# Low-rank factors loaded after batch 0's Q and K, and the last output tile stored in two halves

## The chip, the cores and the metric

The kernel runs on 1 core of one Trainium2 chip. The metric is the device time of the program in microseconds, lower being better; the time given for a kernel is the median of its runs.

## The reference

Sliding-window causal attention over 8 batches, 8 heads, 576 tokens and 64 dimensions a head, and then a mixer: a low-rank product over the tokens and a channel MLP. All inputs and the output are float32.

```python
def _attn_ref(q, k, v):                      # 8, 8, 576, 64
    scores = (1.0 / np.sqrt(D)) * np.matmul(q, k.transpose(0, 1, 3, 2))
    rel = pos[:, None] - pos[None, :]
    scores = np.where((rel >= 0) & (rel < 64), scores, -1000000000.0)
    attn = softmax(scores)
    return np.matmul(attn, v)

def _moe_ref(x, U, V, w_ch1, w_ch2):         # x: 8, 576, 512; U: 576, 32; V: 32, 576
    h = x.transpose(0, 2, 1) @ U @ V
    u = x + h.transpose(0, 2, 1)
    return u + np.maximum(u @ w_ch1, 0.0) @ w_ch2    # 512 -> 2048 -> 512
```

The MLP has by far the most products: 4608 tokens through 512 x 2048 and back.

## The kernel before

All products are in bf16; the loads by POOL's queue (GpSimd) turn float32 into bf16 on the way. Attention goes batch by batch; the MLP goes in 9 chunks of 512 tokens (c = 0 to 8), which don't line up with the batches of 576.

**Attention of a batch.** Q and K are brought into a transposed form, kt and qt: for batches 0 and 1 by TensorE transposes (`TK`, `TQ`, L258, with copies from PSUM at L269 and L274), for batches 2 to 7 by DMA transposes that SP issues (`TX`, L280). `SC(j)` makes the scores of two heads (L311) and their Exp on ScalarE (L329), in batch 0 with the mask added on TensorE (L305). `SC8` does the last block of all heads. `PV(t)` makes the output of token tile t (L364), divided by the sums on VectorE (DVE, L373 and L374) into x. Then comes the low-rank product: `UM` multiplies by U (L396, reading ub) and copies the result to hh on ScalarE (L406); batch 0's `HT` multiplies hh by V (L464, reading vrep), added in PSUM to the transposed x (`XT`, L447), and copies it to uTc, the transposed input of the MLP. `VM` makes the same sum untransposed, un (L486, L499). `UT(t)` transposes a tile of un into uTc where no `HT` did: by TensorE for batches 1 and 2 (L518, copied at L521 by ScalarE), by DMA for the rest (L514).

**MLP of a chunk.** `ch1(i)`, i = 0 to 15, makes 128 hidden channels with 4 matmuls of 512 columns (L560, weights w1b) and a Relu on ScalarE or DVE. `ch2(t, quarter)` sums 16 matmuls of 512 columns for token tile t (L582, weights w2b) into psU; after the fourth quarter DVE adds un (L591) into osb, and SP issues one store of 128 x 512 floats (L594).

**The order.** It is written out by hand. The 32 calls of a chunk's MLP are slots; tables (`PLACE`, `PLACE_1`, `PLACE_2`) say after which slot each piece of the next batch's attention is issued. Chunk 0 carries batch 1, chunk 1 carries batch 2, and so on; in chunk 1, `"VP"` and `"UTP"` place the last steps of batch 1: un (slots 0 to 4) and the transpose of its last tile (slot 5, `"UTP": [5]`). The scores of batch 2 are at slots 6, 6, 9, 9 and 11. Each engine runs its instructions in the order of issue.

**The start.** POOL's queue gets, in order: batch 0's K and Q in two halves of 4 heads each (L117: K, Q, K, Q), its V (L135, L140), the weights w1b in two halves (L211), then copies inside SBUF that shift V (L149, L152), batch 1's Q, K and V, and w2b (L219). SP's queue begins with the low-rank factors: U is loaded twice, in two arrangements of rows (uf0 and uf1, 4 DMAs at L199 to L204), V four times (vf, L208). Batch 0's attention runs alone, before any MLP; `turn_over` puts in matmuls with an unread result (L635). Its order on TensorE is this list, with `SC8` behind it:

```python
    for what in ("K0", "K1", "Q0", "Q1", "S0", "S1", "K2", "K3", "Q2", "Q3", "S2", "S3"):
```

After it, ScalarE casts the factors to bf16:

```python
    for i in range(2):
        nc.scalar.copy(out=ub[i][:], in_=uf[i][:])
    nc.scalar.copy(out=vrep[:, W : W + S], in_=vf[:])
```

and then PV, XT and U of batch 0 follow tile by tile, then the copies of hh, then HT. In batch 0 the copies of K2 and K3 from PSUM and all four of Q are on DVE.

Of the kernel before, what the change touches and what calls it, by code (L numbers as in the profile page):

```python
# [9 lines left out]
ALU = mybir.AluOpType  # L10

BF16 = mybir.dt.bfloat16
FP32 = mybir.dt.float32
# [3 lines left out]
def kernel(  # L17
# [11 lines left out]
    nc = tc.nc  # L29
    B, H, S, D = q.shape  # L30
    DM = H * D
    R = moe_U.shape[1]
    F = moe_w_ch1.shape[1]
    P = nc.NUM_PARTITIONS
    W = 64
# [3 lines left out]
    NFC = F // P  # L39
# [6 lines left out]
    NFULL = S // P  # L46
    CH = 512
    TPC = CH // P
    NTOK = B * S
    NCH = NTOK // CH  # L50
# [6 lines left out]
    outf = out.rearrange("b s m -> (b s) m")  # L57
# [7 lines left out]
    out_pool = ctx.enter_context(tc.tile_pool(name="osb", bufs=4))  # L65
# [3 lines left out]
    psum = {  # L69
        "mm": first.enter_context(tc.tile_pool(name="ps_t0", bufs=2, space=bass.MemoryType.PSUM)),  # L70
        "spare": first.enter_context(tc.tile_pool(name="ps_s0", bufs=1, space=bass.MemoryType.PSUM)),
    }
# [8 lines left out]
    w2b = const.tile([P, NFC, DM], BF16, name="w2b")  # L81
    NT = 5
    uf = [const.tile([P, NT, R], FP32, name=f"uf{i}") for i in range(2)]
    ub = [const.tile([P, NT, R], BF16, name=f"ub{i}") for i in range(2)]
    vrep = const.tile([P, W + S + W], BF16, name="vrep")
    vf = const.tile([P, S], FP32, name="vf")
# [59 lines left out]
    def shift_v(b, copy, tiles):  # L146
# [14 lines left out]
        out=ident[:],  # L161
        in_=ident[:],
# [11 lines left out]
    for n, base, step, mult in ((0, 0, 1, -1), (1, -1, -1, 1), (1, W, 1, -1)):  # L174
        nc.gpsimd.affine_select(
            out=maskA[:, 0, n, :],
            in_=maskA[:, 0, n, :],
# [9 lines left out]
    load_v(0)  # L187
    nc.vector.memset(vrep[:, 0:W], 0.0)
    nc.vector.memset(vrep[:, W + S : W + S + W], 0.0)
    nc.vector.memset(uf[0][:, NT - 1, :], 0.0)  # L190
    nc.vector.memset(uf[1][:, 0, :], 0.0)
    nc.vector.memset(xs[0][W:P, NT - 1, :, :], 0.0)
    nc.vector.memset(xs[1][0:W, 0, :, :], 0.0)
    for i in range(2):
# [1 line left out]
        nc.vector.memset(qn[i][W:P, NFULL, :, :], 0.0)  # L196


    nc.sync.dma_start(  # L199
        out=uf[0][:, 0:NFULL, :], in_=moe_U[0 : NFULL * P, :].rearrange("(c p) r -> p c r", p=P)  # L200
    )
    nc.sync.dma_start(out=uf[0][0:W, NFULL, :], in_=moe_U[NFULL * P : S, :])
    nc.sync.dma_start(out=uf[1][W:P, 0, :], in_=moe_U[0:W, :])
    nc.sync.dma_start(  # L204
        out=uf[1][:, 1:NT, :], in_=moe_U[W:S, :].rearrange("(c p) r -> p c r", p=P)
    )
    for g in range(4):
        nc.sync.dma_start(out=vf[g * R : (g + 1) * R, :], in_=moe_V[:, :])  # L208
    w1v = moe_w_ch1.rearrange("(c p) n -> p c n", p=P)
    for lo, hi in ((0, 1024), (1024, 2048)):  # L210
        nc.gpsimd.dma_start(out=w1b[:, :, lo:hi], in_=w1v[:, :, lo:hi])  # L211
# [11 lines left out]
    u_tiles = {}  # L223
    uT_tiles = {}

    def uT_of(c):
        if c not in uT_tiles:
            uT_tiles[c] = uT_pool.tile([P, TPC, NDC, P], BF16, name="uTc")
        return uT_tiles[c]
# [322 lines left out]
    def mlp(c):  # L552
        uTc = uT_of(c)
        c1 = [None] * NFC

        def ch1(i):
            def f():
                ps = psum["mm"].tile([P, CH], FP32, name="psA", tag="mm")
                for dc in range(NDC):
                    nc.tensor.matmul(  # L560
                        ps[:],
                        w1b[:, dc, i * P : (i + 1) * P],
                        uTc[:, :, dc, :],
                        start=(dc == 0),
                        stop=(dc == NDC - 1),
                    )
                c1[i] = c1_pool.tile([P, CH], BF16, name=f"c1_{i}")
                if i in (DVE_RELU if c > 0 else DVE_RELU_0):
                    nc.vector.tensor_relu(out=c1[i][:], in_=ps[:])  # L569
                else:  # L570
                    nc.scalar.activation(out=c1[i][:], in_=ps[:], func=ACT.Relu)
            return f

        acc = {}

        def ch2(t, quarter):
            def f():
                g = c * TPC + t
                if quarter == 0:
                    acc[t] = psum["mm"].tile([P, DM], FP32, name="psU", tag="mm")  # L580
                for i in range(4 * quarter, 4 * quarter + 4):
                    nc.tensor.matmul(  # L582
                        acc[t][:],
                        c1[i][:, t * P : (t + 1) * P],
                        w2b[:, i, :],
                        start=(i == 0),
                        stop=(i == NFC - 1),
                    )
                if quarter == 3:
                    osb = out_pool.tile([P, DM], FP32, name="osb")  # L590
                    nc.vector.tensor_tensor(  # L591
                        out=osb[:], in0=acc[t][:], in1=u_tiles[g][:], op=ALU.add
                    )
                    nc.sync.dma_start(out=outf[g * P : (g + 1) * P, :], in_=osb[:])  # L594
            return f

        return [ch1(i) for i in range(NFC)] + [ch2(t, r) for t in range(TPC) for r in range(4)]


# [19 lines left out]
    PLACE_2 = {  # L619
        "S": [6, 6, 9, 9, 11],  # L620
        "VP": [0, 1, 2, 2, 3, 4, 4, 4],
        "UTP": [5],
        "PV": [14, 14, 16, 16, 18],
        "TX": [12, 13, 14, 15, 16],
        "U": [19],
# [7 lines left out]
    def turn_over(n, cols=CH):  # L633
        for _ in range(n):
            nc.tensor.matmul(  # L635
                unread[:, 0:cols], idle[:, 0:P], idle[:, 0:cols], start=True, stop=True
            )
# [6 lines left out]
        out=maskA[:, 0, 2, :],  # L644
        in0=maskA[:, 0, 1, :],
# [7 lines left out]
        out=maskA[:, 0, 3:7, :].rearrange("p (o n) w -> p o (n w)", o=2),  # L653
        in_=pair.to_broadcast([P, 2, 2 * W]),
# [3 lines left out]
        out=maskB[:],  # L658
        in0=maskA[:, 0, :, :],
# [5 lines left out]
    for what in ("K0", "K1", "Q0", "Q1", "S0", "S1", "K2", "K3", "Q2", "Q3", "S2", "S3"):  # L665
        j = int(what[1])
        if what[0] == "S":
            a["S"][j]()
        else:
            a["T"][2 * j + (what[0] == "Q")]()  # L670
        turn_over({"K1": 3, "Q1": 1, "S0": 1, "K3": 1, "Q3": 1}.get(what, 0))
    a["S"][HP]()
    nc.vector.tensor_copy(out=maskA[:, 1, :, :], in_=maskA[:, 0, :, :])
# [19 lines left out]
    for c in range(NCH):  # L693
# [32 lines left out]
        for fill, extra in zip(mlp(c) + [lambda: None], slots):  # L726
            fill()
            for f in extra:
                f()
# [30 lines left out]
```

The softmax here doesn't subtract the row's maximum and nothing guards it: scores larger than these inputs give would overflow.

## Time and profile before

| what | value |
|---|---|
| time, median of 3 runs | 329.75 us (329.72 to 330.7) |
| the profiled execution's own time | 330.06 us |
| its span, first to last instruction | 328.3 us |
| busy: TensorE matmul, DVE, ScalarE, POOL | 316.2, 172.2, 94.7, 102.9 us |
| TensorE clock granted, mean | 0.998 |
| chain that ended last, by engine | PE 86%, DVE 5%, ACT 3%, DMA 3% |
| bytes read from and written to HBM | 37.14 MB, 9.44 MB |
| first MLP matmul (L560) | 24.95 us after the span's start |
| last MLP matmul (L582) begins | 324.19 us |

The profile shows one execution. PE is TensorE's matmuls, PEld its weight loads, ACT is ScalarE, SP is the engine that issues stores and transposes; a name with q (SPq, POOLq) is an engine's sequencer, which issues DMAs. Times are microseconds from the start of the span. L12 is line 12 of the kernel. "Busy" is the union of an engine's instructions; a matmul of 512 columns lasts 380 ns, though the next begins 215 ns after it, since they are pipelined. A line of groups or of the timeline gives the start, the length, the engine, the line, output and inputs; in brackets stands the idle time of the engine ahead of it and what ended that. DMA queues: q0 is the queue of POOL, q1 that of SP; for each the page gives packets, megabytes and the share of 16 engines' time.

### The profile page before, as it was taken

How to read it: one execution, taken by the hardware profiler on the slowest of the kernel's cores; microseconds unless marked ns; L12 is line 12 of the kernel's file. 1: busy time of each engine (PE TensorE's matmuls, PEld its weight loads, DVE VectorE, ACT ScalarE, POOL GpSimd, SP SyncE). 2: the span in 40 equal slices, each digit the busy share in tenths (PEclk: the TensorE clock that was granted, in tenths of full speed). 3: DMA queues.
4: the chain of work that ended last, by engine and by line, in shares of the span. 5: the costliest groups of instructions: out<-in, count | busy, mean ns of one | idle time of the engine just before them, and what ended most of it. 6: DMA issues, size and time to landing. Idle time of an engine off the chain costs nothing.

```text
span 328.3 us, 6734 instructions
## 1 busy us (share of the span) xinstructions
PE 316.2 (96%) x2802; PEld 147.9 (45%) x2802; DVE 172.2 (52%) x308; ACT 94.7 (29%) x143; POOL 102.9 (31%) x134
## 2 busy tenths in 40 slices
PE   6889999989999999999999999999999999999995
PEld 2444544434454444444444444444444444444442
DVE  4564682378645844584548553765376425115211
ACT  3435641028223530344025401540063001301400
POOL 8591878536536855417700500000000000000000
PEclk9999999999999999999999999999999999999999
DMA  8999999999999999999996993354300330021011
GB/s 114 179 208 195 170 189 169 148 155 175 131 134 208 165 137 154 207 174 141 145 209 98 134 140 112 62 86 103 105 4 2 73 106 32 2 82 45 0 66 64
DMA packets 151871, 39.56 MB, mean 121 GB/s; under 512 B 140960, under 2 KB 146080, under 8 KB 151840
## 3 DMA queue, kind: packets, MB, share of 16 engines
q0 software_dynamic: 100096, 18.36, 78.9%
q1 hardware_dynamic: 51744, 20.77, 35.5%
q8 instruction: 22, 0.36, 0.5%
q14 instruction: 9, 0.07, 0.1%
HBM read 37.14 MB, written 9.44 MB: 142 GB/s over the span
## 4 chain that ended last, share of the span: by engine, by line
PE 86%; DVE 5%; ACT 3%; DMA 3%; issue 2%; POOL 1%; POOLq 0%
PE psU L582 38%; PE psA L560 34%; PE xr L364 4%; DMA qg<-in_q_dram 3%; PE sc L311 3%; ACT pts L329 3%; PE psv L486 2%; DVE pts L331 1%; PE pshh L396 1%; DVE un L499 1%; PE tpg L258 1%; PE psht L396 0%; PE psh L396 0%; PE tpu L518 0%; PE ua L447 0%
## 5 line engine op out<-in xcount | busy, mean ns | idle before, releaser
L560 PE MATMUL psA<-uTc,w1b 128*128 128x512 bf16 x576 | 133.7, 380 | 2.3 <-DVE uTc L473 0.4
L560 PEld LDWEIGHTS <-w1b 128*128 128x128 bf16 x576 | 53.3, 98 | 63.3 <-issue 2.9
L591 DVE TENSOR_TENSOR osb<-psU,un 128x512 f32<-128x512 f32 x36 | 24.8, 689 | 78.0 <-PE psU L582 78.0
L329 ACT ACTIVATE pts<-sc 128x1024 bf16<-128x1024 f32 x32 | 31.3, 1023 | 8.8 <-PE sc L311 7.3
L331 DVE TENSOR_TENSOR pts<-pts,maskA 128x1024 bf16<-128x1024 bf16 x28 | 19.3, 691 | 10.2 <-ACT pts L329 10.2
L135 POOL DMA_DIRECT2D vA_105<-in_v_dram x16 | 14.1, 885 | 29.4 <-DVE c_9_2735 L569 18.3
L499 DVE TENSOR_TENSOR un<-psv,xs_102 128x512 bf16<-128x512 f32 (+1 forms) x20 | 13.0, 683 | 10.4 <-PE psv L486 10.4
L135 POOL DMA_DIRECT2D vA_104<-in_v_dram x16 | 14.1, 887 | 13.4 <-PE xr L364 7.9
L499 DVE TENSOR_TENSOR un<-psv,xs_103 128x512 bf16<-128x512 f32 (+1 forms) x20 | 13.0, 684 | 8.6 <-PE psv L486 8.4
L364 PEld LDWEIGHTS <-pts 128*64 128x64 bf16 x512 | 11.2, 110 | 10.4 <-issue 4.1
L126 POOL DMA_DIRECT2D kn_108<-in_k_dram x15 | 12.7, 847 | 10.1 <-DMA vA_105<-in_v_dram 5.8
L126 POOL DMA_DIRECT2D qn_110<-in_q_dram x15 | 12.7, 848 | 8.7 <-DMA qn_110<-in_q_dram 4.5
L126 POOL DMA_DIRECT2D kn_109<-in_k_dram x15 | 12.8, 857 | 6.4 <-DMA vA_104<-in_v_dram 3.9
L373 DVE RECIPROCAL rcp<-xr 128x8 f32<-128x8 f32 (+1 forms) x40 | 8.2, 204 | 12.8 <-PE xr L364 12.4
L311 PEld LDWEIGHTS <-kf 64*64 64x64 bf16 x704 | 10.1, 107 | 10.2 <-issue 9.1
L374 DVE TENSOR_TENSOR xs_103<-xr,rcp 128x512 bf16<-128x512 f32 (+1 forms) x20 | 13.8, 692 | 0.7
L374 DVE TENSOR_TENSOR xs_102<-xr,rcp 128x512 bf16<-128x512 f32 (+1 forms) x20 | 13.8, 690 | 0.7
L126 POOL DMA_DIRECT2D qn_111<-in_q_dram x15 | 12.8, 855 | 2.8 <-DMA qn_111<-in_q_dram 2.1
L486 PE MATMUL psv<-hh,vrep 128*128 128x512 bf16 x40 | 12.6, 379 | 0.0
L311 PE MATMUL sc<-qf,kf 64*64 64x128 bf16 (+1 forms) x576 | 11.2, 214 | 0.0
L635 PE MATMUL unread<-idle 128*128 128x512 bf16 x16 | 6.4, 524 | 1.3 <-DVE idle L156 1.3
L364 PE MATMUL xr<-vA_105,pts 128*64 128x65 bf16 x160 | 7.2, 197 | 0.2 <-DVE xs_103 L374 0.2
(553 smaller groups left out, 510.0 us busy)
## 6 DMA issues: line engine op xcount, KB each, us to landing
out_dram<-osb SPq DMA_DIRECT2D x36, 256.0 KB, 3.0
vA_104<-in_v_dram POOLq DMA_DIRECT2D x16, 128.0 KB, 8.1
w1b<-in_moe_w_ch_dram POOLq DMA_DIRECT2D x2, 1024.0 KB, 15.0
vA_105<-in_v_dram POOLq DMA_DIRECT2D x16, 128.0 KB, 11.5
w2b<-in_moe_w_ch_dram POOLq DMA_DIRECT2D x4, 512.0 KB, 12.6
kn_108<-in_k_dram POOLq DMA_DIRECT2D x12, 128.0 KB, 11.9
qn_110<-in_q_dram POOLq DMA_DIRECT2D x12, 128.0 KB, 13.2
kn_109<-in_k_dram POOLq DMA_DIRECT2D x12, 128.0 KB, 10.8
```

The lines of the kernel that those rows point to most:

```text
L126: nc.gpsimd.dma_start(out=dst[0:rows, t, :, :], in_=src[b, :, t * P : t * P + rows, :].rearrange("h p d -> p h d"),)
L135: nc.gpsimd.dma_start(out=va[:, t, :, 0:D], in_=v[b, :, t * P : (t + 1) * P, :].rearrange("h p d -> p h d"),)
L311: nc.tensor.matmul(sc[r0 : r0 + W, g, col * W : (col + n) * W], keys_of(j, u, rs), queries_of(j, blk, n, rs), start=not spare, stop=last o ...
L329: nc.scalar.activation(out=dst, in_=sc[:], func=ACT.Exp, scale=scale)
L331: nc.vector.tensor_tensor(out=dst, in0=dst, in1=maskA.rearrange("p g n w -> p g (n w)"), op=ALU.mult)
L364: nc.tensor.matmul(xr[r0 : r0 + W, h // 4, (h % 4) * VW : (h % 4 + 1) * VW], pts[:, h // 2, h % 2, blk, :] if blk < NB - 1 else ptl[:, h / ...
L374: nc.vector.tensor_tensor(out=x[lo:hi, t, :, :].rearrange("p (a h) d -> p a h d", a=2), in0=xv[:, :, :, 0:D], in1=rcp[lo:hi].to_broadcast( ...
L486: nc.tensor.matmul(ps[0][:, n, :], vrep[:, off : off + P], hh["sb"][:], start=True, stop=True)
L499: nc.vector.tensor_tensor(out=u_tiles[g][rs, :], in0=ps[0][rs, n, :], in1=x[rs, t, :, :].rearrange("p h d -> p (h d)"), op=ALU.add,)
L560: nc.tensor.matmul(ps[:], w1b[:, dc, i * P : (i + 1) * P], uTc[:, :, dc, :], start=(dc == 0), stop=(dc == NDC - 1),)
L582: nc.tensor.matmul(acc[t][:], c1[i][:, t * P : (t + 1) * P], w2b[:, i, :], start=(i == 0), stop=(i == NFC - 1),)
L591: nc.vector.tensor_tensor(out=osb[:], in0=acc[t][:], in1=u_tiles[g][:], op=ALU.add)
```

## The change

Three edits:

- The 8 loads of the low-rank factors on SP are put into `load_low_rank()`, which is called after K3 in the list of the start. It begins with five memsets on DVE that touch uf0, uf1 and vf, so that each load, which writes the same bytes, must wait for DVE to come there. Two of these memsets stood at the start before; three are of one column only. The casts on ScalarE stay where they were.
- `"UTP": [5]` becomes `[7]`: the TensorE transpose of batch 1's last tile comes two slots later in chunk 1.
- The last token tile of the last chunk goes through `ch2_last`: two accumulations of 256 columns, one after the other, instead of one of 512; each half is added by DVE and stored by two DMAs of 64 rows, one issued by SP and one by ScalarE.

```diff
-    nc.vector.memset(uf[0][:, NT - 1, :], 0.0)
-    nc.vector.memset(uf[1][:, 0, :], 0.0)
...
-    nc.sync.dma_start(
-        out=uf[0][:, 0:NFULL, :], in_=moe_U[0 : NFULL * P, :].rearrange("(c p) r -> p c r", p=P)
-    )
...
+    def load_low_rank():
+        for part in (uf[0][:, NT - 1, :], uf[0][:, 0, 0:1], uf[1][:, 0, :], uf[1][:, 1, 0:1], vf[:, 0:1]):
+            nc.vector.memset(part, 0.0)
+        nc.sync.dma_start(
+            out=uf[0][:, 0:NFULL, :], in_=moe_U[0 : NFULL * P, :].rearrange("(c p) r -> p c r", p=P)
+        )
+        nc.sync.dma_start(out=uf[0][0:W, NFULL, :], in_=moe_U[NFULL * P : S, :])
+        nc.sync.dma_start(out=uf[1][W:P, 0, :], in_=moe_U[0:W, :])
+        nc.sync.dma_start(
+            out=uf[1][:, 1:NT, :], in_=moe_U[W:S, :].rearrange("(c p) r -> p c r", p=P)
+        )
+        for g in range(4):
+            nc.sync.dma_start(out=vf[g * R : (g + 1) * R, :], in_=moe_V[:, :])
...
+        def ch2_last(t, quarter):
+            def f():
+                g = c * TPC + t
+                half = quarter // 2
+                cs = slice(half * DM // 2, (half + 1) * DM // 2)
+                if quarter % 2 == 0:
+                    acc[half] = psum["mm"].tile([P, DM // 2], FP32, name="psL", tag="mm")
+                for i in range(8 * (quarter % 2), 8 * (quarter % 2) + 8):
+                    nc.tensor.matmul(
+                        acc[half][:],
+                        c1[i][:, t * P : (t + 1) * P],
+                        w2b[:, i, cs],
+                        start=(i == 0),
+                        stop=(i == NFC - 1),
+                    )
+                if quarter % 2 == 1:
+                    osb = out_pool.tile([P, DM], FP32, name="osb")[:, 0 : DM // 2]
+                    nc.vector.tensor_tensor(
+                        out=osb, in0=acc[half][:], in1=u_tiles[g][:, cs], op=ALU.add
+                    )
+                    for r0, queue in ((0, nc.sync), (W, nc.scalar)):
+                        queue.dma_start(
+                            out=outf[g * P + r0 : g * P + r0 + W, cs], in_=osb[r0 : r0 + W, :]
+                        )
+            return f
...
         def ch2(t, quarter):
+            if c == NCH - 1 and t == TPC - 1:
+                return ch2_last(t, quarter)
...
-        "UTP": [5],
+        "UTP": [7],
...
             a["T"][2 * j + (what[0] == "Q")]()
+        if what == "K3":
+            load_low_rank()
```

Where times are told of the kernel after the change, its lines are counted in its own file: L258 is L261 there, L269 L272, L274 L277, L329 L332, L396 L399, L406 L409, L464 L467, L560 L563, L675 L709, L676 L710, the first load L201 and the loads of V L210; the last tile's add and stores are L596 and L600.

More of the change, by code (lines that the diff above doesn't have):

```diff
@@ L196 @@
         nc.vector.memset(qn[i][W:P, NFULL, :, :], 0.0)
-    nc.sync.dma_start(
-        out=uf[0][:, 0:NFULL, :], in_=moe_U[0 : NFULL * P, :].rearrange("(c p) r -> p c r", p=P)
-    )
[L202 to L208, printed above, removed]
+    def load_low_rank():
[11 more added lines that the diff above has]
+            nc.sync.dma_start(out=vf[g * R : (g + 1) * R, :], in_=moe_V[:, :])
     w1v = moe_w_ch1.rearrange("(c p) n -> p c n", p=P)
```

## Prediction

> **What bounds the kernel now.** I read the page's shares first (PE busy 96% of 328.3 us), then the chain of waits: TensorE carries 86% of it. From 26 to 300 us the waits of TensorE hold one of 1.1 us, five of 0.4 and one of 0.2. So only three places can give time: the start, that one wait, and the end. For the start I read the chain in order of time:
>
> ```profile
> 3.87 8.90 DMA qg<-in_q_dram
> 12.77 0.04 issue
> 12.81 0.45 PE tpg L258 x12
> ...
> 23.05 0.38 ACT hh L406
> 23.43 0.05 issue
> ```
>
> To be exact on the second half of that stretch, the timeline of the engines concerned (start, length, engine, line) says more:
>
> ```profile
> 0.81 0.45 SPq L199 DMA_DIRECT2D uf_95<-in_moe_U_dram  x1
> 3.97 2.24 SPq L208 DMA_DIRECT2D vf<-in_moe_V_dram  x4
> 11.41 1.42 DVE L269 COPY kf<-tpm 128x576 bf16<-128x576 bf16 x2 [1.42 <-PE tpm L258]
> 13.30 0.76 DVE L274 COPY qf<-tpg 128x576 bf16<-128x576 bf16 x1 [0.46 <-PE tpg L258]
> 16.97 0.34 ACT L675 CAST ub_97<-uf_95 128x160 bf16<-128x160 f32 x1
> 17.41 0.69 ACT L676 CAST vrep<-vf 128x576 bf16<-128x576 f32 x1
> 23.05 0.65 ACT L406 CAST hh<-psh 128x256 bf16<-128x256 f32 x2 [4.95 <-PE psh L396]
> ```
>
> The second half of Q ends the first wait at 12.77. The three casts of the low-rank factors need data by 16.97, and two later things need the casts: the first U product (L396) at 19.89, and the copy of hh at 23.05, which stands behind the three casts on ScalarE. Today the loads are issued from 0.81 to 6.2 us and nobody waits for them.
>
> The DMA issues by window, put side by side, tell how the two queues share the engines (q0 is POOL's, q1 is SP's; windows 7.25 to 8.75, 74 to 76.5 and 17 to 24 us):
>
> ```profile
> q0 software_dynamic: 356, 0.26, 113.9%
> q1 hardware_dynamic: 343, 0.04, 35.6%
> ...
> q0 software_dynamic: 1044, 0.13, 80.0%
> q1 hardware_dynamic: 1043, 0.26, 79.4%
> ...
> q0 software_dynamic: 731, 1.46, 111.7%
> ```
>
> Where both queues have work they move one packet each in turn, whatever the sizes. And from 17 to 24 us, POOL's queue moves w1b alone: 731 packets in 7 us, so on each of 16 engines one 2 KB packet per 0.153 us.
>
> **What the Trainium skill says.** "DMA: Bandwidth & Descriptors", section "Queues, rings and completion order": each DMA engine goes round robin between the queues it has work for, draining a packet from one before it switches. The counts above agree. Its section "Issuing engines are not separate DMA queues" says that a second issuing engine saves issue time only; the trace of before has no issue from ScalarE, so nothing here shows it. "TensorE: Matmul & The Clock Gate", Part 1, says that an idle stretch of about 3.4 us halves the clock, and that as long a busy one restores it. The trace agrees on the slow start: the first nine 512-column matmuls take 4.02 us, 0.43 each, against 0.215 later.
>
> **Part 1, the held loads.** Two memsets move and three small ones come in, on DVE behind K3's copy. All 8 loads on SP wait for them; they pass nothing on SP, whose next work is a store at 52 us, and nothing on POOL.
> - *What it gives.* Without the 1152 packets of U (576 rows, twice) and 128 of V, the 16 engines have less to do before Q lands. Packets of U cost little (in the 7.25 to 8.75 window q0 kept 237 a microsecond, against 248 from 4.5 to 6.5), those of V some 0.1 us each: (640 x 0.007 + 128 x 0.1)/16 = 1.1 us per engine (estimate; the first 512 of U went before Q and K began). So Q lands near 11.5. But DVE then sets the time: K3's copy ends at 12.83 and the 5 memsets stand next, spaced 0.05 us, about 0.25. Q2's copy starts at 13.1, not 13.30. With some 0.1 to 0.2 of the first halves the gain is 0.35 us, bounds 0 and 0.5.
> - *What it costs.* The memsets end near 12.9 and SP issues the loads until about 17.3 (8 issues from 0.42 to 0.73, as before). The first load had its packets 1.1 us after its issue, so packets start at 14.0. By then POOL's queue has w1b: it began at about 14.5 to 16.5 and comes 1.1 earlier. Each engine has 64 of its packets (2 x 512 over 16), and 72 of U with 8 of V against them. In turn: 64 x (0.153 + 0.007) = 10.2 us for the first 64, the other 16 beside batch 1's K and Q (0.07 a pair) 1.2 us, landing 0.4: V is in at **25.8**. That is the lower end. Before, the loads were slower than one for one: from 3.2 us (second issue and 1.1) to the last landing at 12.5 they took 9.3 us, 143 packet times of K and Q (0.065) where 48 would do. With 143 + 32 (the first load was free then) packet times, 64 at 0.16 and 111 at 0.065, V is in at 14.0 + 10.2 + 7.2 = **31.4**, the upper end. I take the middle, **28.6**.
> - *Who waits.* The first U product needs two loads, 36 packets per engine: 14.0 + 36 x 0.16 + 0.4 = 20.2 at least, near 22 in the middle case, plus the cast 0.34, instead of 19.89. TensorE, in order, holds batch 0's last PV tiles behind it. Then ScalarE waits for V, casts (0.69), and only then copies hh: 28.6 + 0.7 = 29.3 instead of 23.05, **+6.3 us** (+3.4 to +9.1). HT and the whole first MLP stand behind. The idle stretch may cool TensorE's clock: half of 3.4 us is 1.7 at most, I take **+1.0**. The part's gain of 0.35 goes under in this wait.
>
> **Part 2, one transpose two slots later.** The waits show what stands there:
>
> ```profile
> PE tpu L518 <- DVE un L499: 1.1, 1, 1.1
> PEld L311 <- DMA qf<-qn_110: 0.4, 1, 0.4
> ```
>
> At slot 7, 2 matmul groups and 2 scores later, un is long done: **-1.1 us**. The copy of tpu on ScalarE comes behind two Exp (1.94 us), but chunk 2 alone needs it. The cover to watch is the second line: scores of batch 2, right behind, need the transposes of tile 3, issued at 64.85 and landing 8.9 us later, at 73.7; TensorE comes at 73.59. If TensorE were not late, it would find them missing and get 0 to 0.5 of the 1.1. With TensorE 7 us late and POOL's loads not late, the transposes have less beside them, and I count it whole.
>
> **Part 3, the last tile in halves.** TensorE does 32 matmuls of 256 columns for 16 of 512, the same columns; the weight loads, 98 ns each, lie under 108 ns. No cost (0.1 at most). DVE's last add has 256 columns: 0.69 for 512 and 0.20 for a reciprocal of 8 give 0.96 ns a column, 0.44, so -0.25. The last store:
>
> ```profile
> 324.61 0.69 DVE L591 TENSOR_TENSOR osb<-psU,un 128x512 f32<-128x512 f32 x1 [2.76 <-PE psU L582]
> 325.32 0.33 SPq L594 DMA_DIRECT2D out_dram<-osb  x1
> ```
>
> It landed 2.0 us after its issue. Half the bytes from two queues: I take -0.35, bounds 0 (latency alone) and -0.6. An issue from ScalarE isn't in the trace; SP's took 0.33, I take the same. The first half's stores lie beside the second half's matmuls. Sum **-0.6** (-0.2 to -0.9).
>
> **Sum.** The profiled execution took 330.06, its span 328.3 and 1.8 around it: 330.06 + 6.3 + 1.0 - 1.1 - 0.6 = 335.7. The median shown, 329.75, is 0.3 lower: **335.4 us**.
>
> **The rivals.** *A: the loads land in time.* For: U's packets are small, and a free queue landed the first load in 2.0 us. Against: every SP load or store issued beside a busy POOL queue took 4.7 us or more. It decides by V's landing: before 22 us nobody waits, and the end is the other one: 0.35 and 0.6 gained, with 0 to 1.1 of part 2, 327.7 to 328.8, likeliest 328.5, faster. *B: a shallow wait.* Landings take about 7 us from issue, as before: V in at 24, hh copied at 24.7, +1.6; less 0.6 and 0.5 to 1.1, 329.6 to 330.3, no change. *C: worse than the middle.* V at 31.4 and a cold clock: 329.75 + 9.1 + 1.7 - 1.7 = 338.8; loads strictly one after the other would give 340.
>
> **How the numbers follow.** The forecast, from its lower end (329.75 + 3.4 - 1.7 = 331.5) to C, has 0.74; A 0.14, B 0.12. A measurement of this kernel tells 0.3%, 1.0 us, from no change: below 328.76 is faster, above 330.74 slower. A gives faster 0.13, B and the edges 0.11 of no change, the rest, 0.76, is slower. The likeliest case alone has 331.5 to 339; the range for 8 in 10 takes in B and half of A: 328.8 to 339.5.
>
> **What would show it.** Right: packets of q1 beside w1b from 14 us on; V's landing after 25; ScalarE idle before the casts at L709 and L710 by DMA uf and vf; TensorE idle at L399 and before L409; no wait at tpu; the last add 0.44. Wrong: casts done before 22 us and hh copied before 23.05. A single late wait at hh with no wait at the U product would mean that U's loads pass quickly and V's alone are late.

## The result, and the profile after

The changed kernel takes **339.21 us** (median of 4 runs, 337.89 to 340.48), beside 330.23 (329.72 to 331.37) for the kernel before in the same comparison: ratio **1.0267, interval 1.0209 to 1.0324**. The forecast was 335.4, with a range of 328.8 to 339.5. It is slower, as forecast, and near the upper end: the medians are 9.0 us apart, where +5.6 was forecast.

The profiled execution took 340.48 us, the longest of the four, its span 338.8. Set beside the 328.3 of before, the 10.5 us (1.5 more than between the medians) can be counted from milestones of the two timelines (us from the start of the span):

| milestone | before | after | later by | added in this stretch |
|---|---|---|---|---|
| ScalarE copies hh (L406, now L409) | 23.05 | 31.11 | 8.06 | 8.06 |
| first MLP matmul, chunk 0 | 24.95 | 33.44 | 8.49 | 0.43 |
| chunk 1's first | 64.77 | 73.93 | 9.16 | 0.67 |
| chunk 2's first | 101.54 | 111.84 | 10.30 | 1.14 |
| chunk 3's first | 135.21 | 145.32 | 10.11 | -0.19 |
| last matmul ends | 324.57 | 334.72 | 10.15 | 0.04 |
| end of the span | 328.32 | 338.78 | 10.46 | 0.32 |

Chunks 3 to 6 take 33.48 us each in both, chunk 7 27.6. So the loss lies where the change reaches: in the start, in the first two chunks, and in the tail.

The clock on the page of before and on that of after, and the chain by engine after:

```profile
PEclk9999999999999999999999999999999999999999
...
PEclk9955999999999999999999999999999999999999
...
PE 73%; DMA 13%; DVE 3%; issue 3%; POOL 3%; ACT 2%; SPq 1%; POOLq 0%; ACTq 0%
```

DMA has gone from 3% to 13% of the chain, and slices 3 and 4, which are 17 to 34 us, have TensorE at half its clock; before it was 9 throughout. The chain in order of time (start, length, what):

```profile
2.16 5.50 DMA qg<-in_q_dram
...
17.91 12.53 DMA vf<-in_moe_V_dram
30.53 0.67 ACT vrep L710
31.21 0.55 ACT hh L409 x2
...
33.44 1.70 PE psA L563 x4
```

The chain no longer ends its first stretch on the second half of Q (3.87 to 12.77 before, landing at 11.27 now). It goes through the last load of V: issued at 17.91, landed 12.5 us later, then its cast, then hh, as the prediction's order has it. The waits of TensorE (total, times, longest):

```profile
PE psh L399 <- ACT ub_97 L709: 4.3, 1, 4.3
PE sc L314 <- DMA qf<-qn_110: 2.4, 1, 2.4
PE uam L467 <- ACT hh L409: 2.0, 1, 2.0
...
PE xr L367 <- issue: 1.0, 1, 1.0
```

and those of ScalarE from 0 to 45 us:

```profile
ACT ub_97 L709 <- DMA uf_95<-in_moe_U_dram: 8.2, 1, 8.2
...
ACT ub_98 L709 <- DMA uf_96<-in_moe_U_dram: 4.1, 1, 4.1
...
ACT vrep L710 <- DMA vf<-in_moe_V_dram: 1.4, 1, 1.4
```

Two waits in the start, at the U product and at hh, both behind ScalarE, which waits for the loads. The wait at tpu, the tile of the transpose that was moved (1.1 before), is gone, and one of 2.4 at batch 2's scores stands in its place. The DMA queues from 18 to 21 us, in the window of w1b:

```profile
q0 software_dynamic: 311, 0.61, 106.7%
q1 hardware_dynamic: 311, 0.04, 16.5%
```

311 packets each: one for one, 2 KB against 128 bytes. On 16 engines this is 3 x 16 / 311 = 0.154 us a pair, what one w1b packet took alone (0.153): U's packets are nearly free, but each waits for a packet of w1b. The issue list gives the rest: SP issued the loads from 12.53 to 18.33; the first packets of q1 came only at 16.5; U landed at 23.42, 24.26, 25.00 and 28.73, V at 29.25 to 30.43. Before, U had landed by 10.76 and V by 12.50.

The end, from the timeline of the engines concerned:

```profile
334.75 0.42 DVE L596 TENSOR_TENSOR osb<-psL,un 128x256 f32<-128x256 f32 x1 [1.32 <-PE psL L587]
...
335.20 0.48 SPq L600 DMA_DIRECT2D out_dram<-osb  x1
...
335.21 0.50 ACTq L600 DMA_DIRECT2D out_dram<-osb  x1
```

The add took 0.42 for 0.69. But the two issues took 0.48 and 0.50 for 0.33, the later store landed 2.22 us after its issue (2.01 before), and the span ended 1.35 after that landing (0.99 before). From the last matmul to the end, which is called the tail below, it is 4.07 us, before 3.75.

### The profile page after: what moved, and what is told of

It reads as the page before. It is cut to its first block, busy times and chain, and to the rows that moved or that the text cites. A ratio compares the mean times of both kernels' runs of the same rounds, so it can differ in the third digit from the quotient of the medians.

```text
span 338.8 us, 6755 instructions
## 1 busy us (share of the span) xinstructions
PE 317.8 (94%) x2795; PEld 151.2 (45%) x2818; DVE 171.5 (51%) x312; ACT 94.8 (28%) x143; POOL 102.3 (30%) x134
## 4 chain that ended last, share of the span: by engine, by line
PE 73%; DMA 13%; DVE 3%; issue 3%; POOL 3%; ACT 2%; SPq 1%; POOLq 0%; ACTq 0%
PE psA L563 32%; PE psU L614 29%; DMA vf<-in_moe_V_dram 4%; DMA qf<-qn_110 3%; PE xr L367 3%; PE sc L314 3%; DMA qn_111<-in_q_dram 2%; PE psv L489 2%; DMA uTc<-un 2%; ACT pts L332 2%; DMA qg<-in_q_dram 2%; PE psL L587 1%; DVE pts L334 1%; POOL kn_109 L126 1%; PE pshh L399 1%
## 5 line engine op out<-in xcount | busy, mean ns | idle before, releaser
L563 PE MATMUL psA<-uTc,w1b 128*128 128x512 bf16 x576 | 134.3, 381 | 1.9 <-DVE c_5_1799 L572 0.4
L563 PEld LDWEIGHTS <-w1b 128*128 128x128 bf16 x576 | 53.5, 98 | 63.2 <-issue 3.2
L623 DVE TENSOR_TENSOR osb<-psU,un 128x512 f32<-128x512 f32 x35 | 24.1, 690 | 75.2 <-PE psU L614 75.2
L332 ACT ACTIVATE pts<-sc 128x1024 bf16<-128x1024 f32 x32 | 31.3, 1023 | 11.9 <-PE sc L314 11.6
L502 DVE TENSOR_TENSOR un<-psv,xs_103 128x512 bf16<-128x512 f32 (+1 forms) x20 | 13.1, 686 | 8.6 <-PE psv L489 8.4
L367 PEld LDWEIGHTS <-pts 128*64 128x64 bf16 x512 | 11.8, 114 | 11.4 <-issue 5.2
L126 POOL DMA_DIRECT2D qn_110<-in_q_dram x15 | 12.9, 861 | 7.2 <-DMA vA_105<-in_v_dram 4.9
L126 POOL DMA_DIRECT2D qn_111<-in_q_dram x15 | 13.3, 883 | 1.3 <-DMA vA_104<-in_v_dram 0.9
L367 PE MATMUL xr<-vA_104,pts 128*64 128x65 bf16 x160 | 6.8, 203 | 1.3 <-issue 1.0
L367 PE MATMUL xr<-vA_105,pts 128*64 128x65 bf16 x160 | 7.2, 197 | 0.2 <-DVE xs_103 L377 0.2
## 6 DMA issues: line engine op xcount, KB each, us to landing
w1b<-in_moe_w_ch_dram POOLq DMA_DIRECT2D x2, 1024.0 KB, 14.6
```

The source lines that it names most:

```text
L126: nc.gpsimd.dma_start(out=dst[0:rows, t, :, :], in_=src[b, :, t * P : t * P + rows, :].rearrange("h p d -> p h d"),)
L332: nc.scalar.activation(out=dst, in_=sc[:], func=ACT.Exp, scale=scale)
L367: nc.tensor.matmul(xr[r0 : r0 + W, h // 4, (h % 4) * VW : (h % 4 + 1) * VW], pts[:, h // 2, h % 2, blk, :] if blk < NB - 1 else ptl[:, h / ...
L502: nc.vector.tensor_tensor(out=u_tiles[g][rs, :], in0=ps[0][rs, n, :], in1=x[rs, t, :, :].rearrange("p h d -> p (h d)"), op=ALU.add,)
L563: nc.tensor.matmul(ps[:], w1b[:, dc, i * P : (i + 1) * P], uTc[:, :, dc, :], start=(dc == 0), stop=(dc == NDC - 1),)
L623: nc.vector.tensor_tensor(out=osb[:], in0=acc[t][:], in1=u_tiles[g][:], op=ALU.add)
```

## The experiments

The theory: the loss is in the held loads, which meet w1b and take turns with it packet by packet; the other two parts bring nothing. The rivals: the loss comes from another part; the loads are late because SP issues them late; the clock, not the wait, costs the time. The median of the kernel before differs from one comparison to the next (330.23, 332.0, 331.66, 331.28), so kernels are compared by their ratio to it within one. The first MLP matmul and the tail, told below, are those of each run's profiled execution. That execution is now a run's fastest and now its slowest, so the totals are judged by the ratio, and the traces are read for their waits.

### Each part alone

**Held loads only** (to the changed kernel):

```diff
-        "UTP": [7],
+        "UTP": [5],
...
-            if c == NCH - 1 and t == TPC - 1:
-                return ch2_last(t, quarter)
```

> Only the held loads are changed; the transpose of batch 1's last tile and the last output tile stay as before. Theory (the loads pass one for one with w1b and TensorE waits for the casts): V lands near 30.4, first MLP matmul near 33.4 as against 24.95, and as the scores of batch 2 wait for late DMA transposes only where the transpose's own wait doesn't hide it, the whole loss is here: 8 to 10 us slower than before, about the changed kernel's time less 0.3. Rival (the transpose's new place costs on its own, through the 2.4 us wait at the scores): 6 to 8 us slower only.

338.74 us, ratio 1.0242 (1.0191 to 1.0294). First MLP matmul at 32.73, tail 3.75, the wait at tpu back with its 1.1, none at the scores. The held loads alone have a loss of the same size (1.0267 above, 1.0233 in the repetition below); what the other two parts bring together is too small for these totals to tell.

**One transpose two slots later, only** (to the kernel before):

```diff
-        "UTP": [5],
+        "UTP": [7],
```

> Only the transpose of batch 1's last tile goes from slot 5 to slot 7. Theory (the scores behind it need DMA transposes that land at 73.7, and the old wait hid that): the 1.1 us wait at the transpose is gone and one of about 1.2 us on a DMA transpose stands at the first scores of batch 2 instead; the time is within 0.3 us of before. Rival (the wait was a pure loss, as the prediction counted it): 1.1 us faster.

331.69 us, ratio 0.9987 (0.9962 to 1.0011): not told apart from before, but the interval would hold the forecast's 1.1 us (0.3%) as well, so the trace has to say more. There is no wait at tpu, and 0.3 at the first scores of batch 2, where 1.2 was expected. From chunk 1's first matmul to chunk 2's it took 35.81 us for 36.77: 0.96 gained. But the next chunk took 34.66 for 33.67, 0.99 more, because of a new wait in its first part, from the waits of TensorE in this run:

```profile
PE psA L560 <- DMA uTc<-un: 1.0, 1, 1.0
```

This is a chunk's MLP waiting for the DMA transpose of un into uTc. Over the two chunks nothing is left of the gain. That the later transpose brings this wait with it is not shown: the next run, which leaves the transpose in its place, has the same wait with 0.8, and other runs with the old place have 0.3 or none.

**Halves only** (to the kernel before, `ch2_last` of the diff, nothing else):

> Only the last tile is computed and stored in two column halves. Theory from the changed kernel's trace (last add 0.27 shorter; issue to landing 2.2 instead of 2.0; eight waits of SP behind the landing instead of two): last matmul's end to the span's end 4.0 to 4.1 us instead of 3.76, so 0.2 to 0.4 us slower than before. Rival (the prediction's sum): 0.6 us faster.

331.43 us, ratio 0.9994 (0.997 to 1.0017). The tail is 4.07, to the hundredth that of the changed kernel; 0.32 is below what the total can show. In chunks 1 and 2 it has the 1.1 at tpu, as before, and also

```profile
PE psA L560 <- DMA uTc<-un: 0.8, 1, 0.8
```

so this wait does not need the transpose at slot 7.

### What makes the loads late

**Released after Q1 in place of K3** (to the changed kernel):

```diff
-        if what == "K3":
+        if what == "Q1":
             load_low_rank()
```

> The changed kernel with the held loads let go after Q1's copy instead of K3's, about 3 us earlier. Theory (what costs is w1b's 2 KB packets beside the loads): they now pass beside the 128-byte packets of batch 0's V, 0.03 us or less each, V of the factors lands before 20, no wait at the U product or at hh, Q's second half still lands near 11.5: first MLP matmul 24.3 to 24.7; with the end's 0.3 lost, within 0.5 us of before. Rival (holding the loads behind DVE in itself makes them late, through SP's issue and the memsets): still 3 us or more slower than before.

339.91 us, ratio 1.024 (1.0196 to 1.0284): nothing regained in the median. SP issued from 9.52, 3.0 us earlier, and the first packets came at 13.1, still 3.6 us after the issue. U's first three landed by 20.19, but the fourth at 26.24 and V at 26.91 to 28.05: the rest met w1b. The waits of TensorE show which load counts:

```profile
PE uam L467 <- ACT hh L409: 5.7, 1, 5.7
...
PE psh L399 <- ACT ub L709: 0.6, 1, 0.6
```

The wait at the U product shrank to 0.6, and that at hh grew to 5.7. V decides, and V is last in the queue. In this execution, the fastest of the six (336.99), the first MLP matmul came at 31.06, 2.4 us before the changed kernel's; the median shows none of it. An earlier issue helps little while the loads still end beside w1b.

**w1b issued behind the V copies of POOL** (to the changed kernel):

```diff
+    for t in range(NFULL):
+        shift_v(0, nc.gpsimd.tensor_copy, range(t, t + 1))
     for lo, hi in ((0, 1024), (1024, 2048)):
         nc.gpsimd.dma_start(out=w1b[:, :, lo:hi], in_=w1v[:, :, lo:hi])
-    for t in range(NFULL):
-        shift_v(0, nc.gpsimd.tensor_copy, range(t, t + 1))
```

> The changed kernel with POOL's two loads of w1b issued behind the seven copies that shift V, so that no big packets stand beside the held loads. Theory (w1b's packets hold them up): the low-rank loads land by 18 to 19 us instead of 24.3 and 30.4, no wait at the first U product, hh copied by 22.5; w1b's first half lands near 24.5 and may hold the first MLP matmul for up to 1 us; first MLP matmul 24 to 25.5 and the time within 1.5 us of before. Rival (SP's loads are late from their issue on): V still lands after 25 and the first MLP matmul comes after 28.

335.36 us, ratio 1.0116 (1.0062 to 1.0169): about half of the loss is gone. U, issued from 14.20, landed at 17.18 to 20.84, 2.0 to 3.6 us after the issue where the changed kernel took 10.9 and more; no wait at the U product. V, issued from 17.85, met w1b again from about 19 and landed at 22.19 to 26.00, with a wait of 4.0 at hh. The first MLP matmul came at 28.58. By the signs set down beforehand this is the rival's outcome (V after 25, the first MLP matmul after 28), and the theory's times were missed by far. But the rival has all loads late, and U was not: the loads that ran ahead of w1b's packets landed soon, those that met them late.

**w1b in packets of 512 bytes** (to the changed kernel):

```diff
-    for lo, hi in ((0, 1024), (1024, 2048)):
-        nc.gpsimd.dma_start(out=w1b[:, :, lo:hi], in_=w1v[:, :, lo:hi])
+    for lo in range(0, 1024, 256):
+        nc.gpsimd.dma_start(out=w1b[:, :, lo : lo + 256], in_=w1v[:, :, lo : lo + 256])
     for t in range(NFULL):
         shift_v(0, nc.gpsimd.tensor_copy, range(t, t + 1))
+    for lo in range(1024, 2048, 256):
+        nc.gpsimd.dma_start(out=w1b[:, :, lo : lo + 256], in_=w1v[:, :, lo : lo + 256])
```

> The changed kernel with w1b loaded in eight transfers of 256 columns (packets of 512 bytes) in place of two of 1,024 columns (packets of 2 KB), four of them ahead of batch 0's V copies on POOL and four behind. Packet theory: the SP queue and the POOL queue pass one packet each in turn whatever their sizes, so smaller packets beside U's let U pass sooner. In the changed kernel a pair took 0.154 us (311 pairs in 3 us on 16 engines); with 512 bytes in place of 2 KB about 0.06, so U's 1,152 packets take some 4.3 us from their first at 16.5 in place of some 11: U's last lands near 21 (19.5 to 22.5) where it was 28.73, V's factor near 22.5 (21 to 24.5) where it was 30.43, the first MLP matmul comes near 26 (24.5 to 28) where it was 33.44, and the time is 331 to 334. Byte theory (the queues share bytes, or the loads are late because SP issues them late): U's last after 27, V's factor after 28.5, first MLP after 31.5 and the time 337 or more.

332.66 us, ratio 1.0048 (1.0028 to 1.0067), beside 1.0233 for the unaltered changed kernel in the same comparison. SP issued even later, from 14.36, and no packet of q1 came before 18 us; but then U was in by 23.01 and V by 24.71 (expected by 22.5 and 24.5 at the latest), and the first MLP matmul came at 27.29. The queues from 18 to 21 us in this run:

```profile
q0 software_dynamic: 937, 0.46, 115.4%
q1 hardware_dynamic: 1002, 0.18, 48.2%
```

In the same 3 us q1 passes 1,002 packets in place of 311, while the bytes of both queues together are the same, 0.64 and 0.65 MB. This kernel holds the loads even longer, and POOL's queue has packets in every microsecond beside them; w1b's packets are smaller. (Its second half is also issued behind POOL's copies, from 18.37; that alone was not tried.) Of the loss of 8.0 us (339.26 - 331.28) 6.6 are gone. That settles it against "SP issues late" and against sharing by bytes: the loads wait for their turn, and a turn is as long as the other queue's packet. The turn is not strictly one for one here: from 18 to 19 us it was 373 to 153 (q1's first packet came at 18.3), from 20 to 21 it was 233 to 458; why was not tried.

**U on POOL's queue, V held on SP** (to the kernel before):

```diff
-    nc.sync.dma_start(
+    nc.gpsimd.dma_start(
         out=uf[0][:, 0:NFULL, :], in_=moe_U[0 : NFULL * P, :].rearrange("(c p) r -> p c r", p=P)
     )
...
+        if what == "K3":
+            nc.vector.memset(vf[:, 0:1], 0.0)
+            for g in range(4):
+                nc.sync.dma_start(out=vf[g * R : (g + 1) * R, :], in_=moe_V[:, :])
```

All four loads of U stand on POOL between batch 0's V and w1b.

> The kernel before with U's four loads in POOL's queue between batch 0's V and w1b, and only V's four on SP, behind K3's copy. Theory (a load in the queue of the big packets stands ahead of them and pays nothing in turn; eight packets an engine from SP cost little): Q's second half lands near 11.5 instead of 12.8, U by 16, V near 19 to 20, no wait at the U product or at hh; first MLP matmul 24.0 to 24.5; 0.3 to 0.8 us faster than before. Rival (the four issues on POOL, 3 us, delay the shifts of V, and these hold PV): first MLP matmul after 25 and slower.

332.39 us, ratio 1.0025 (1.0007 to 1.0044). All loads were in by 19.51 and Q's second half landed at 11.41, so the collision is avoided, and there is no wait at the U product and 0.4 at hh. Yet the first MLP matmul came at 26.03 where 24.0 to 24.5 was expected, and the time is 0.25% longer than before: the theory missed. The rival's sign (after 25) is there, but not its cause, since TensorE waits for no shift of V in the start; it waits 1.7 us at "xr <- issue". In this trace, the slowest of 22, chunk 2 also waits 1.5 for a shift of V on DVE ("psA <- DVE vB").

### The clock

**TensorE kept busy ahead of the U product** by idle matmuls (to the changed kernel), run in two comparisons, the second time beside the changed kernel itself:

```diff
             a["XT"][t - 2]()
+            if t == 2:
+                a["idle"](9)
             a["U"][t - 2]()
```

> The changed kernel with 36 matmuls of zeros (128 columns, added to the open sums, so that nothing changes) ahead of the first U product, where TensorE waits 4.3 us. Theory (part of the loss is TensorE's clock, 0.5 from 17 to 34 us in the changed kernel): the clock is full again by the first MLP matmul, HT and the first MLP run at 0.215 us a matmul, and the time is 1 to 2 us under the changed kernel's. Rival (the clock doesn't matter, since loads set the end): within 0.3 us of the changed kernel.

337.80 us, ratio 1.0204 (1.0149 to 1.0258); the first four MLP matmuls at full clock, at 32.79. That is 1.4 us under the changed kernel's 339.21, which comes from another comparison; so both were run again side by side.

> The changed kernel unaltered, on one chip with the next kernel, as its partner. 337.5 to 340, some 1.024 of before; first MLP matmul 33.4, its four matmuls 1.70 us.

339.26 us (337.93 to 340.95), ratio 1.0233 (1.0197 to 1.027).

> The changed kernel with more idle matmuls between the last scores of batch 0's tile and the waits, as in the run of this kind before, now beside the unaltered changed kernel on the same chip. If the low clock after the wait costs what the first MLP matmuls show, it is 0.6 to 1.5 us shorter than the changed kernel, and first MLP comes near 32.8; if the clock's dip lies inside waits that go on anyway, within 0.4 of it. In both cases over 4 us longer than before, since the loads land as late.

339.88 us (338.0 to 340.33), ratio 1.0242 (1.0214 to 1.027): no gain beside its partner. The idle matmuls do not keep the clock up for certain. Of the table by windows (us, busy times of the engines, clock, DMA share, GB/s) two rows of this second run:

```profile
25.00:29.00 4.00, 4.00 (x42) 2.03 (x41) 1.78 (x4) 0.24 (x1) 0.76 (x1) 0.57 1.34 237
...
33.00:37.00 4.00, 4.00 (x14) 1.57 (x13) 1.42 (x3) 1.19 (x2) 2.29 (x4) 0.69 3.08 138
```

The clock is 0.57 after the wait at the U product, and 0.69 once more in the MLP. In the changed kernel's repetition it was 1.00 from 33 us on, and its first MLP matmul came 1.90 us after hh, as before. So the clock's cost differs from one execution to the next, and the experiment did not isolate it. The traces set side by side do price it: chunk 0 takes 39.81 to 40.22 us in the ten executions that begin its MLP at full clock, and 40.49 to 41.22 in the four that begin it at half (the changed kernel, the release after Q1, w1b later, and this second run).

### The last tile by one queue

**Halves by one queue** (to the kernel before, with `ch2_last`, but):

```diff
-                    for r0, queue in ((0, nc.sync), (W, nc.scalar)):
-                        queue.dma_start(
-                            out=outf[g * P + r0 : g * P + r0 + W, cs], in_=osb[r0 : r0 + W, :]
-                        )
+                    nc.sync.dma_start(out=outf[g * P : (g + 1) * P, cs], in_=osb)
```

> The kernel before with the last tile in two column halves, each half stored by one DMA of 128 rows from SP. Theory (the add is 0.27 shorter; what took that back in the two-queue form is two slower issues, a landing 0.2 later and eight waits of SP behind it): last matmul's end to the span's end 3.4 to 3.5 us, against 3.76 before and 4.07 in the two-queue form; 0.3 us faster than before, near what can be told. Rival (half a tile's DMA lands as late whatever the queue, and the waits stay behind it): 3.7 us or more.

330.98 us, ratio **0.9977 (0.9955 to 0.9998)**: faster than before by 0.2%, which the interval only just tells from none. The tail is 3.14: the add 0.42, an issue of 0.33, landing 1.72 us after it. The split in columns was good; the split in rows between two queues, which were tried only together, was not. "DMA: Bandwidth & Descriptors" of the Trainium skill, section "Rules for kernel authors", says of two transfers to disjoint partition halves that one of 128 partitions is to be used, since both go over the same 16 engines. The halves by two queues and by one agree: tail 4.07 against 3.14.

**384 columns, then 128, by one queue** (to the last kernel; the tiles of the sum and of osb get the same width):

```diff
-                cs = slice(half * DM // 2, (half + 1) * DM // 2)
+                cs = slice(0, 3 * DM // 4) if half == 0 else slice(3 * DM // 4, DM)
```

> The kernel before with only its last output tile altered: 384 columns and then 128, each stored by SP alone in one transfer. Halves by one queue had a tail of 3.14 us from the last matmul to the end (before 3.75). If the add goes with the columns, the second part's add and transfer are shorter again: tail near 2.95 (2.8 to 3.1), time 0.6 to 1.0 under before, ratio 0.997. If the issue and the landing have a floor, the tail is 3.1 to 3.2 as with halves; if packets of 512 bytes land slower than those of 1 KB, 3.2 to 3.6.

330.75 us, ratio **0.9978 (0.996 to 0.9997)**. Its end, from the timeline:

```profile
326.55 0.96 SPq L597 DMA_DIRECT2D out_dram<-osb  x2
326.86 0.29 DVE L594 TENSOR_TENSOR osb<-psL,un 128x128 f32<-128x128 f32 x1 [0.34 <-PE psL L585]
```

The last add takes 0.29, its store landed 1.66 us after its issue (327.18), the tail is 2.94. That 0.20 over equal halves is seen in the tail alone; the two totals do not tell them apart. Both beat the changed kernel, and the kernel before by 0.2%.

## Why the prediction was right, and where it was off

**What bounds the start: right.** Q's second half no longer ends the first wait; V's last load does, through its cast and hh, as in the order given. Of the signs listed as "right" all are there, save that q1's packets beside w1b begin at 16.5 and not at 14.

**First packets at 14.0: wrong.** I took 1.1 us from issue to packets, from a load on a free queue. Here it took 4.0, and 3.5 to 4.2 in all seven traces in which w1b was queued on POOL by then; with w1b later it was 1.1. So the packets came 2.5 us after 14.0, the largest miss of part 1. Why the start takes so long is open. SP's issues were mis-sized too: one of the eight took 1.65 in place of 0.73 at most, but the packets of U ahead of V's were not through until 28.73, so this cost nothing here.

**Turns with w1b: right in kind, near in size in part by luck.** The packets went one for one, at 0.154 a pair, which the forecast had as its lower end (11.8 us from the first packet to V's landing); I took the middle between it and a slower turn (17.4), 28.6 - 14.0 = 14.6. It took 30.43 - 16.5 = 13.9, but the rest over one for one came only at the end: from 27 to 29 us, with V's packets of 2,304 bytes left, q1 passed 137 to q0's 398. (The 0.007 us for a packet of U does not come out of the two rates named for it, 16/237 - 16/248 = 0.003; 0.154 against 0.153 shows even less.) So V was 1.8 late against 28.6 (2.5 - 0.7), and hh came at 31.11 in place of 29.3: +8.06 for +6.3, inside the bounds of +3.4 to +9.1. The U product came at 24.75 in place of some 22, for the same late first packets.

**Cold clock, +1.0 (1.7 at most): near in size in this one execution, but not as argued.** The clock was at half from 17.78 for 17.1 us, five times the 3.4 of the Trainium skill's "TensorE: Matmul & The Clock Gate", Part 1, so half of 3.4 was no bound. It fell before TensorE came to the first wait for a load (20.44), after a stop of 1.0 within the PV matmuls (16.12 to 17.12). Much of it lies inside waits; 0.43 between hh and the first MLP matmul and 0.67 in chunk 0 are left, 1.1 in sum. In the repetition the clock fell at 23.87, inside the wait, and was full again at 30.70, before hh: both were nil. The 1.0 should have been a bound and not a part of the sum.

**Part 2, -1.1: wrong.** The step that failed is "with TensorE 7 us late and POOL's loads not late, the transposes have less beside them". On SP the transposes of batch 2 stand behind the MLP's first store, which waits for DVE's add and so for TensorE's first finished tile: the store was issued at 61.43 for 52.27, the transposes began at 61.99 for 52.84, 9.15 later, and tile 3 landed at 83.92 for 73.71, 10.2 later, while TensorE, without its wait at tpu, came to the scores only 8.0 later (81.58 for 73.59). They moved with the engine that they were thought to run ahead of. The timeline of TensorE there, with its wait in brackets:

```profile
83.96 0.50 PE L314 MATMUL sc<-qf,kf 64*64 64x128 bf16 x24 [2.38 <-DMA qf<-qn_110]
```

The cover that the prediction named as the one to watch was the right one; I should have counted it. How much it takes differs: 2.4 here, 0.9 in the repetition, 0 to 1.1 in the other kernels with held loads and slot 7. Chunks 1 and 2 together took 71.39 in the changed kernel's trace, 0.95 more than before, but 69.95 in the repetition, 0.49 less; with the held loads and the old slot they took 70.18. So where 1.1 was to be gained, one execution lost 0.95 and the other gained 0.49, or 0.2 against the held loads alone.

**Part 3, -0.6: wrong, by sign.** The add is right (0.42 for an estimate of 0.44). The store's -0.35 was wrong: +0.32 in all, and all eight traces with two queues have a tail of 4.05 to 4.07. "Half the bytes from two queues" sets a landing against bytes, while the landing came 0.21 later after the issue, 0.17 of it by the longer issue itself, and 0.36 more passed from the landing to the end, where eight waits on semaphores of 0.06 each stand on SP (two before). With one queue the term is -0.61, just the forecast size: the right number for another kernel.

**The sum.** Forecast +6.3 + 1.0 - 1.1 - 0.6 = +5.6; measured in the profiled execution +8.06 + 1.10 + 0.95 + 0.32 + 0.04 = +10.5. The repetition, set beside the same trace of before, has +8.35 up to hh, nothing for the clock, -0.49 in chunks 1 and 2, +0.32 in the tail, +8.2 in all. So the late V is in both, and the clock and part 2's +0.95 belong to the first alone. Rival C (338.8) came nearest, though not by its own terms: V was not as late as 31.4, but parts 2 and 3 did not bring the 1.7 that it still credited; its nearness is luck. Rivals A and B fell with V's landing after 25. A further weakness: the sum stands on one execution of before, with its first MLP matmul at 24.95. With the same start, the runs here had it at 24.95 (halves by two queues), 26.31 (by one), 27.04 (384 and 128) and 28.10 (transpose later). With the loads held behind K3 and w1b unaltered it came within 32.68 and 33.44, since V's landing sets it. So the same change, set beside another execution of the old start, would have cost up to 3 us less at this place.

## What to carry to other kernels

A small load held back because it is "off the critical path" met a big one in another queue here. Before holding one back, look at what stands in the other queues when it will come: count its packets and not its bytes, price each at the other queue's packet, and allow for a late first one (here 4.0 us after the issue, on a free queue 1.1). If it must be late, make the large transfer's packets smaller or put it behind. Taking away a wait of an engine pays only as far as what its next steps need comes earlier too: here most of a wait of 1.1 us, or more than all of it, came back as a wait for transposes that had moved with the engine. And of the last store, a short last piece of columns from one queue gave 0.2%; halving its rows between two queues as well made the tail longer, 4.07 in place of 3.14.

## What the runs showed of the hardware that I had not expected

- A load from SP had its first packet 3.5 to 4.2 us after its issue in the seven traces in which w1b was queued on POOL, and 1.1 where POOL's queue was free or just running dry. A full queue is not all of it: with U on POOL and w1b not yet issued, the first two packets came after 1.6, beside a full stream of 128-byte packets. The cause is open.
- In the start, TensorE stops within the PV matmuls of batch 0 (L364, "xr <- issue"), where no data are missing: 0.6 us before, 1.0 after, 0.4 to 1.8 in thirteen of the fourteen traces, none over 0.3 in the run with w1b later. In every trace a packet of 16 KB on a queue of kind "instruction" (q8) is under way ahead of that place for 1.0 to 1.9 us beside the data queues, and in the thirteen TensorE goes on 1.3 to 1.7 us after its end. A second such packet, later in the start, has no stop behind it. It may be that the fetch of instructions is held up by the loads, and this would limit what an earlier Q can give, and explain part of the spread of the start; the two were seen together and not tried apart. In five of the thirteen, with stops of 1.0 to 1.8 us, the clock fell to half within 1.2 us after the stop; in the other eight, with stops of up to 1.3, it did not.
- Halving the rows of a store between SP and ScalarE made each issue dearer: 0.48 to 0.58 us against 0.33 for one of 128 rows.
